# Gated linear attention with a hardswish feed-forward: alpha, k and q of three chunks loaded two tokens to a partition and turned by products

## The chip, the cores and the metric

The kernel runs on one core of one Trainium2 chip. The metric is device time in microseconds (us), the median of a few runs. The kernel before takes 530.95 us (three runs, 530.88 to 531.62).

## What is computed

```python
# attention: batch 4, 8 heads, 768 tokens, head size 48
for t in range(S):
    state = alpha[:, :, t, :, None] * state + np.einsum('bhd,bhe->bhde', k[:, :, t], v[:, :, t])
    y[:, :, t] = np.einsum('bhd,bhde->bhe', q[:, :, t], state)
# then, on 3072 tokens of 384 numbers
h = x @ w_in                       # 384 x 2048
g = h * np.clip(h + 3.0, 0.0, 6.0) / 6.0
return g @ w_out                   # 2048 x 384
```

The inputs alpha, k, q and v lie in memory as batch, head, token, head element, in float32. One token of one head is therefore a run of 48 numbers, 192 bytes, and the next token of the same head follows it directly. The two weight matrices come as float64 and are rounded to float32 on the chip from their bits.

## The kernel before

The tokens are worked off in 24 chunks of 128, six to a batch entry. For one chunk, alpha, k and q are wanted with the head elements along the partitions: a pair of heads takes 128 partitions (64 for each head, 48 of them used), four pairs stand side by side, and the 128 tokens run along the free axis. In memory the tokens come first, so each of the three has to be turned.

For chunks 0 to 5 (`FIRST = 6`) this is done on TensorE. `load_akq` (L253, its DMA at L256) fetches one tensor of one chunk with one DMA, token by token: partition s holds token s, eight heads of 64 columns each, of which 48 are filled with a run of 192 bytes. The other 16 columns hold a constant that is set once (L91: one for alpha, zero for k and q). The buffers are a ring of three for each tensor (`rings`). `transposed` (L276, the instruction at L284) then turns it with four transposes of 128 by 128, each for a pair of heads, into one bank of PSUM. From chunk 6 on, loads of runs of 640 and 768 bytes (L264) and transposes on VectorE (L288) take their place.

What follows for one chunk: ScalarE copies the turned alpha out of PSUM (`place_alpha`, L302). VectorE makes two running products of it with scans (L311 `decay`, L322 `growth`) and multiplies the turned k and q by them (`scaled`, L334). TensorE turns k back to token order (`k_by_token`, L393), ScalarE copies that (L397). Products of k with v give the update of the state (`update`, L452), which VectorE adds (L460, L462); ScalarE puts the state into its place (L438). Products of k with q give the scores (L365), VectorE masks them (L375), and `attend` (L478) makes the chunk's result, which ScalarE copies out (L487) for the feed-forward (L512, L501, L539 for the first tokens, L623 and L726 later).

Two features set the order. First, everything stands in one list written out by hand (from L774), with `manual_schedule`; each engine gets its instructions in that order and works them in that order. A word names a step and its arguments. The list begins:

```python
z.0.5 z.0.3 z.0.1 qa.0.0 w.0 d2.0 d3.0 la.0 ta.0.0 z.0.8 lk.0 tk.0.1 la.1 ta.1.2
lq.0 tq.0.3 lk.1 lv.0.0 d1.0 ca.0 r.0 p.0 k.0 kb.0.0 z.0.2 z.0.2 q.0 la.2 dx.0 ca.1
r.1 ck.0 u.0.2.1 sm.0.0 qa.0.1 sv.0.1 tk.1.0 p.1 sc.0.2.3 w.2 lq.1 sm.0.1 k.1 m.0
ta.2.0 z.0.2 d1.2 ca.2 d2.2 kb.1.0 ck.1 r.2 tq.1.2 q.1 dx.2 lv.1.1 u.1.3.1 z.0.3
```

Here `la`, `lk`, `lq` and `lv` are the loads of alpha, k, q and v, and `w` one of 768 KB of weights. `ta`, `tk` and `tq` are the turns. `ca` is the copy of alpha, `r` and `p` the scans, `k` and `q` the products of L334. `kb` and `ck` bring k back to token order, `u` is the update. `sc` and `m` are scores and mask, `d1` to `d4` the rounding of weights. `z.0.8` is eight products of the identity with itself that nobody reads (`idle`, L555). The last number of a turn is its PSUM bank.

Second, all loads and stores are issued by SyncE (SP), one after the other. Each DMA signals one of eight semaphores, taken in turn, and the issue of a DMA waits until the DMA that had this semaphore before, eight issues earlier, has landed.

Of the kernel before, what the change touches and what calls it, by code (L numbers as in the profile page):

```python
# [17 lines left out]
def kernel(  # L18
# [32 lines left out]
    nc = tc.nc  # L51
    B, H, S, D = q.shape
# [10 lines left out]
    HB = C // 2  # L63
# [9 lines left out]
    ident = consts.tile([C, C], FP, tag="ident")  # L73
# [10 lines left out]
    NR = 3  # L84
    NV = 3
    ring = {}
    rings = consts.tile([C, 3 * NR, H, 64], FP, tag="rings")
    for r in range(NR):
        for name, pad in (("a", 1.0), ("k", 0.0), ("q", 0.0)):
            t = ring[name, r] = rings[:, 3 * r + "akq".index(name)]  # L90
            (nc.vector if r == 0 else nc.gpsimd).memset(t[:, :, D:64], pad)  # L91

    vs, As = [], []
    for r in range(NV):
        t = consts.tile([C, 2, H, 64], FP, tag=f"v{r}", name=f"v{r}")
# [10 lines left out]
    for r in range(2):  # L106
        t = consts.tile([C, NP * W + 1], FP, tag=f"ax{r}")
        nc.vector.memset(t, 0.0)
        aX.append(t)
        t = consts.tile([C, NP * W], FP, tag=f"ini{r}")  # L110
# [118 lines left out]
    def bank(name, j, i):  # L229
        ps_t[name, j] = banks[i].rearrange("r (p n) -> r p n", p=NP)  # L230
        return ps_t[name, j]
# [7 lines left out]
    for r in range(NQ):  # L239
        for name in "akq":  # L240
            quads[name, r] = consts.tile([C, NP, V, D], FP, tag=f"{name}q{r}",
                                         name=f"{name}q{r}")

    def rows(t, j):
        b, c = divmod(j, NC)
        return t[b, :, c * C : (c + 1) * C, :]

    def pad(r):
        for name in "akq":
            for o in (BLK, 3 * BLK):  # L250
                nc.gpsimd.memset(quads[name, r][o : o + BLK, :, V - 1, D - BLK : BLK], 1.0)

    def load_akq(name, j):  # L253
        src = rows({"a": alpha, "k": k, "q": q}[name], j)
        if j < FIRST:
            nc.sync.dma_start(out=ring[name, j % NR][:, :, 0:D],  # L256
                              in_=src.rearrange("h s d -> s h d"))
            return
        to = quads[name, j % NQ]
        to = to.rearrange("r p v d -> r p (v d)")  # L260
        t = src.rearrange("(p a) (u v) d -> a u p (v d)", a=2, v=V)
        for o in range(4):
            skip = BLK * (o % 2)
            nc.sync.dma_start(out=to[BLK * o : BLK * (o + 1), :, 0 : V * D - skip],  # L264
                              in_=t[o // 2, :, :, skip : V * D])
# [10 lines left out]
    def transposed(name, j, i=None):  # L276
        if j >= FIRST:
            t = (K_t if name == "k" else Q_t)[j] = (Ks if name == "k" else Qs)[j % 2]
            by_blocks(t, name, j)
            return  # L280
        t = bank("t" + name, j, i)
        src = ring[name, j % NR]
        for p in range(NP):
            nc.tensor.transpose(  # L284
                t[:, p], src[:, 2 * p : 2 * p + 2].rearrange("s h d -> s (h d)"), ident)

    def by_blocks(to, name, j):
        nc.vector.transpose(out=to.rearrange("r p (u v) -> r p v u", v=V),  # L288
                            in_=quads[name, j % NQ][:, :, :, 0:BLK])
# [305 lines left out]
    for i in range(8):  # L595
        r, o = divmod(i, 3)
# [70 lines left out]
    t = {1: b[0, 1], 2: spare[:, 0], 3: spare[:, 1], 4: spare[:, 2]}  # L667
# [76 lines left out]
    def store2(g, i):  # L744
# [5 lines left out]

    steps = {
        "la": lambda j: load_akq("a", j), "lk": lambda j: load_akq("k", j),
        "lq": lambda j: load_akq("q", j), "lv": load_v, "pd": pad, "w": load_weight,
        "d1": round_low, "d2": magnitude, "dx": sign, "d3": high_bits, "d4": add_low,
        "ta": lambda j, *i: transposed("a", j, *i), "tk": lambda j, *i: transposed("k", j, *i),
        "tq": lambda j, *i: transposed("q", j, *i), "ca": place_alpha, "r": decay, "p": growth,
        "k": lambda j: scaled("k", j), "q": lambda j: scaled("q", j),
        "sc": scores, "m": masked, "sp": scores_of_two, "mp": masked_two, "up": update_two, "qa": place_q, "kb": k_by_token, "ck": keep_k,
# [197 lines left out]
```

## Time and profile before

| | |
|---|---|
| median of 3 runs | 530.95 us |
| the profiled execution | 531.43 us |
| its span (first to last instruction) | 529.6 us |
| TensorE (PE) busy | 519.6 us, 98% of the span |
| VectorE (DVE) busy | 471.4 us, 89% |
| ScalarE (ACT) busy | 256.9 us, 48% |
| GpSimd (POOL) busy | 49.2 us, 9% |
| granted clock of TensorE | 1.00 in every stage |
| DMA | 124,100 packets, 54.40 MB, mean 103 GB/s |
| loads of alpha, k, q into the ring (L256) | 18 DMAs of 192 KB |

PE is TensorE's matmul and PEld its weight loads. In a list of instructions the columns are start, duration, engine, line, operation, output and input, count, and in brackets the idle time before it with what ended it. A matmul's recorded duration reaches past the start of the next one, so the time that it takes up is read from the distance of starts. A product in float32 stands there as two matmuls, a transpose as one.

### The profile page before, as it was taken

The page shows a single profiled execution, that of the slowest core. Times are in us where ns is not written, and L with a number is a line of the kernel's source. Part 1 is how long each engine was busy: PE and PEld are TensorE (multiplying, and loading weights), DVE is VectorE, ACT ScalarE, POOL GpSimd, SP SyncE. Part 2 cuts the span into 40 slices and gives each one's busy share as a digit, 9 for nine tenths or more (in the row PEclk, how much of TensorE's full clock was granted, in tenths as well). Part 3 has the DMA queues.
Part 4 walks back from the last instruction along what each step waited for, and adds up shares of the span by engine and source line. Part 5 has one row for each costly group of instructions (what it writes and reads, how often), then busy time and mean ns, then how long its engine had stood idle before and what let it go on. Part 6 is the DMA issues. An engine that isn't in the chain of part 4 may idle for free.

```text
span 529.6 us, 15031 instructions
## 1 busy us (share of the span) xinstructions
PE 519.6 (98%) x6300; PEld 496.0 (94%) x6300; DVE 471.4 (89%) x817; ACT 256.9 (48%) x503; POOL 49.2 (9%) x71
## 2 busy tenths in 40 slices
PE   7899999999999999999999999999999999999997
PEld 6688887789999999999999999999999999999997
DVE  7999999999999999999999999999999996376381
ACT  5789867013564443553353562554344534443320
POOL 7323343100000000000000000001000000000000
PEclk9999999999999999999999999999999999999999
DMA  9999989300416535456415356463435041000011
GB/s 172 221 251 266 249 239 198 71 15 1 106 22 139 125 81 118 117 123 139 100 30 133 85 108 152 95 138 87 83 82 123 15 77 37 2 24 1 1 39 45
DMA packets 124100, 54.40 MB, mean 103 GB/s; under 512 B 83328, under 2 KB 116864, under 8 KB 124032
## 3 DMA queue, kind: packets, MB, share of 16 engines
q1 hardware_dynamic: 124032, 53.44, 44.8%
q8 instruction: 49, 0.80, 0.7%
q14 instruction: 19, 0.16, 0.1%
HBM read 44.50 MB, written 8.91 MB: 101 GB/s over the span
## 4 chain that ended last, share of the span: by engine, by line
PE 87%; DVE 7%; DMA 2%; ACT 2%; issue 1%; POOL 0%; SPq 0%; DVEq 0%; ACTq 0%
PE m_ps L726 36%; PE m_ps L623 33%; PE m_ps L501 6%; PE m_ps L539 4%; PE t_ps L478 4%; PE t_ps L365 2%; PE t_ps L452 2%; DMA v<-in_v_dram 1%; DMA rings<-in_alpha_dram 1%; DVE R L311 1%; DVE A L353 1%; ACT raw L191 1%; DVE k L288 1%; PE m_ps L512 1%; DVE k L334 0%
## 5 line engine op out<-in xcount | busy, mean ns | idle before, releaser
L726 PE MATMUL m_ps<-w,g_sb 128*128 128x192 f32 x704 | 122.2, 327 | 0.0
L629 ACT COPY g_sb<-m_ps 128x512 f32<-128x512 f32 x110 | 63.6, 583 | 110.7 <-PE m_ps L623 82.5
L726 PEld LDWEIGHTS m_ps<-w,g_sb 128*128 128x128 f32 x704 | 113.9, 190 | 0.7
L726 PE MATMUL m_ps<-rings,g_sb 128*128 128x192 f32 x528 | 91.3, 326 | 0.0
L726 PEld LDWEIGHTS m_ps<-rings,g_sb 128*128 128x128 f32 x528 | 85.4, 190 | 0.0
L623 PE MATMUL m_ps<-xc,w 128*128 128x128 f32 x640 | 83.2, 278 | 0.4 <-DVE oh L742 0.2
L517 ACT ACTIVATE r<-g_sb,half 128x512 f32<-128x512 f32 x80 | 57.2, 723 | 47.2 <-DVE g_sb L564 19.0
L623 PEld LDWEIGHTS m_ps<-xc,w 128*128 128x128 f32 x640 | 77.5, 191 | 1.8 <-DVE oh L742 0.4
L521 DVE SCALAR_TENSOR_TENSOR g_sb<-r,g_sb 128x512 f32<-128x512 f32 x80 | 54.0, 683 | 6.3 <-ACT r L517 5.3
L623 PE MATMUL m_ps<-xT,raw 128*128 128x128 f32 x400 | 52.5, 277 | 0.0
L623 PEld LDWEIGHTS m_ps<-xT,raw 128*128 128x128 f32 x400 | 48.5, 192 | 0.2
L670 DVE TENSOR_TENSOR g_sb<-g_sb 128x512 f32<-128x512 f32 (+1 forms) x55 | 41.9, 788 | 2.8 <-PE m_ps L726 2.7
L428 POOL TENSOR_TENSOR st<-sm,R 128x192 f32<-128x192 f32 x20 | 11.9, 595 | 342.4 <-DVE sm L462 338.5
L385 ACT COPY A<-q 48x256 f32<-48x256 f32 x88 | 35.5, 404 | 14.6 <-DVE q L334 13.3
L623 PE MATMUL m_ps<-xT,w 128*128 128x128 f32 x320 | 42.0, 277 | 0.0
L623 PEld LDWEIGHTS m_ps<-xT,w 128*128 128x128 f32 x320 | 38.9, 192 | 0.2 <-ACT g_sb L629 0.2
L501 PE MATMUL m_ps<-xT,w 128*128 128x256 f32 x144 | 32.6, 382 | 0.0
L623 PE MATMUL m_ps<-xc,raw 128*128 128x128 f32 x240 | 32.1, 277 | 0.0
L311 DVE TENSOR_TENSOR_SCAN R<-t,ones 128x516 f32<-128x516 f32 x24 | 29.9, 1247 | 0.4 <-ACT t L302 0.3
L501 PEld LDWEIGHTS m_ps<-xT,w 128*128 128x128 f32 x144 | 26.8, 190 | 3.6
L623 PEld LDWEIGHTS m_ps<-xc,raw 128*128 128x128 f32 x240 | 29.9, 191 | 0.3
L560 DVE TENSOR_TENSOR g_sb<-g_sb 128x512 f32<-128x512 f32 x40 | 26.9, 682 | 3.4 <-ACT g_sb L629 3.1
(105 smaller groups left out, 716.9 us busy)
## 6 DMA issues: line engine op xcount, KB each, us to landing
raw<-in_moe_w_out_dram SPq DMA_DIRECT2D x8, 768.0 KB, 5.4
raw<-in_moe_w_in_dram SPq DMA_DIRECT2D x6, 768.0 KB, 6.9
v<-in_v_dram SPq DMA_DIRECT2D x48, 96.0 KB, 3.4
out_dram<-oh SPq DMA_DIRECT2D x44, 96.0 KB, 1.8
far<-kq SPq DMA_DIRECT2D x64, 64.0 KB, 2.2
kb<-far SPq DMA_DIRECT2D x64, 64.0 KB, 2.1
qq<-in_q_dram SPq DMA_DIRECT2D x36, 96.0 KB, 2.6
aq<-in_alpha_dram SPq DMA_DIRECT2D x36, 96.0 KB, 2.7
```

Source lines behind the costliest of these rows:

```text
L311: nc.vector.tensor_tensor_scan(out=reverse(R, n - 1, n), data0=reverse(ax, n, n), data1=reverse(ones, n, n), initial=0.0, op0=ALU.mult, op ...
L385: nc.scalar.copy(out=to[:, a], in_=Q_t[j][64 * a : 64 * a + D, :, half])
L478: nc.tensor.matmul(y_of(j, (i + 1) // 2, p)[:, HB * b : HB * b + HB], vb[:, p, e : e + 32], A_t[j][:, b, 2 * p + a], start=(b == 0 and i = ...
L501: nc.tensor.matmul(h[:, f], w1[:, kk, o : o + C], xT_t[g][:, kk], start=(kk == 0), stop=(kk == KT - 1))
L517: nc.scalar.activation(out=to, in_=h, func=AF.Relu, bias=half, scale=1.0 / 6.0)
L521: nc.vector.scalar_tensor_tensor(out=to, in0=r, scalar=1.0, in1=h, op0=ALU.min, op1=ALU.mult)
L539: nc.tensor.matmul(o_t[c], gs[0][:, f, c * C : (c + 1) * C], w2[:, f], start=(f == 0), stop=(f == NF - 1))
L560: eng.tensor_tensor(out=out, in0=in0, in1=in1, op=ALU.add if s1 > 0 else ALU.subtract)
L623: nc.tensor.matmul(acc[g][i][:, f * C : (f + 1) * C], spots[w][:, f * C : (f + 1) * C], x_of(g, x), start=(first and f == 0), stop=last, s ...
L629: nc.scalar.copy(out=slots[z], in_=acc[g][i])
L670: nc.vector.tensor_tensor(out=out, in0=in0, in1=in1, op=ALU.subtract)
L726: nc.tensor.matmul(to[g], a, rhs[:, f], start=(first and f == 0), stop=(last and f == HF - 1), skip_group_check=True)
```

## The change

For chunks 0, 1 and 2 (`PAIRS`), alpha, k and q are loaded two tokens to a partition: token 2u and 2u+1 of a head go together, as one run of 384 bytes, to partition u (heads 0 to 3) or 64+u (heads 4 to 7). This is one DMA for each group of four heads, so two DMAs of 96 KB take the place of one of 192 KB, with 512 runs in the place of 1024. A partition now holds 384 numbers side by side, and the constant columns stand behind them (the memset at L91 has the same size and another place).

The turn of such a tensor is no longer four transposes but eight products with the identity. Each has 64 columns of the loaded data as its stationary operand (48 of one head and one token parity, and 16 that belong to what follows and are not used), and the identity of 128 columns as its moving one. Its result has 64 partitions and 128 columns: two groups of four heads, 64 token pairs each. It is written to every second column of the PSUM bank, so that the bank is laid out as it was. Consecutive products go to the lower and the upper 64 partitions in turn. Everything that reads the bank is as before, and so is the list. Chunks 3 to 5 keep the old load and the old turn.

```diff
             t = ring[name, r] = rings[:, 3 * r + "akq".index(name)]
-            (nc.vector if r == 0 else nc.gpsimd).memset(t[:, :, D:64], pad)
+            (nc.vector if r == 0 else nc.gpsimd).memset(t[:, 6:8], pad)
...
+    PAIRS = {("a", 0), ("k", 0), ("q", 0), ("a", 1), ("k", 1), ("q", 1), ("a", 2), ("k", 2), ("q", 2)}
+
     def load_akq(name, j):
         src = rows({"a": alpha, "k": k, "q": q}[name], j)
+        if (name, j) in PAIRS:
+            to = ring[name, j % NR].rearrange("r h e -> r (h e)")
+            t = src.rearrange("(g i) (u x) d -> g u i (x d)", g=2, x=2)
+            for g in range(2):
+                nc.sync.dma_start(
+                    out=to[HB * g : HB * g + HB, 0 : 8 * D].rearrange("u (i e) -> u i e", i=4),
+                    in_=t[g])
+            return
         if j < FIRST:
             nc.sync.dma_start(out=ring[name, j % NR][:, :, 0:D],
                               in_=src.rearrange("h s d -> s h d"))
...
         t = bank("t" + name, j, i)
         src = ring[name, j % NR]
+        if (name, j) in PAIRS:
+            flat = src.rearrange("s h e -> s (h e)")
+            for n in range(2):
+                for x in range(2):
+                    for a in range(2):
+                        to = t[64 * a : 64 * a + 64].rearrange("r (g n) (u x) -> r n x g u", g=2, x=2)
+                        o = D * (2 * (2 * n + a) + x)
+                        nc.tensor.matmul(to[:, n, x], flat[:, o : o + 64], ident,
+                                         start=True, stop=True)
+            return
         for p in range(NP):
             nc.tensor.transpose(
```

## Prediction

> **What bounds the kernel now.** First the slices of the whole span (the page's second part), then the chain of waits of the start, then the instructions in order of time.
>
> ```profile
> PE   7899999999999999999999999999999999999997
> DVE  7999999999999999999999999999999996376381
> DMA  9999989300416535456415356463435041000011
> ```
>
> A slice is 13 us. PE is full from the third slice on, so what happens in the first two decides when this full stretch begins. DMA is full there too, which makes shorter loads look welcome. The busy times in stretches of 5 us (PE, PEld, DVE, ACT, POOL, clock, DMA share, GB/s) ask whether anyone waits for them:
>
> ```profile
> 10.00:15.00 5.00, 4.19 (x87) 3.38 (x85) 4.96 (x7) 2.63 (x7) 4.36 (x12) 1.00 1.30 236
> 15.00:20.00 5.00, 2.55 (x26) 1.93 (x18) 4.79 (x10) 3.73 (x6) 0.85 (x4) 1.00 1.28 220
> 20.00:25.00 5.00, 4.96 (x149) 4.57 (x150) 4.23 (x9) 3.85 (x9) 1.34 (x1) 1.00 1.12 210
> ```
>
> From 10 to 20 us DVE is busy 9.75 of 10 us: DVE bounds the start, not DMA. The chain of waits shows the one place where a load counts after the first:
>
> ```profile
> 13.08 6.92 DMA v<-in_v_dram
> 20.00 0.04 issue
> 20.04 0.57 PE t_ps L452 x30
> ```
>
> The second half of v of chunk 1 lands at 20.00, PE waits for it, and DVE for PE:
>
> ```profile
> 6.97 0.63 PE L284 MATMUL t_ps<-ident,rings 128*128 128x128 f32 x4 [1.54 <-DMA rings<-in_alpha_dram]
> 7.44 1.95 PE L555 MATMUL m_ps<-ident 128*128 128x128 f32 x16
> 9.23 1.04 PE L284 MATMUL t_ps<-ident,rings 128*128 128x128 f32 x8
> ...
> 10.59 0.63 PE L284 MATMUL t_ps<-ident,rings 128*128 128x128 f32 x4 [0.32 <-DMA rings<-in_q_dram]
> ...
> 11.47 0.68 DVE L334 TENSOR_TENSOR q<-t_ps,P 128x512 f32<-128x512 f32 x1
> 12.07 1.64 DVE L311 TENSOR_TENSOR_SCAN R<-t,ones 128x516 f32<-128x516 f32 x1
> ...
> 17.73 1.23 DVE L311 TENSOR_TENSOR_SCAN R<-t,ones 128x516 f32<-128x516 f32 x1
> ...
> 19.21 0.69 DVE L334 TENSOR_TENSOR q<-t_ps,P 128x512 f32<-128x512 f32 x1
> ...
> 20.72 0.36 DVE L462 TENSOR_TENSOR s<-t_ps,st 128x192 f32<-128x192 f32 x1 [0.81 <-PE t_ps L452]
> ```
>
> From 6.57 to 19.9 DVE goes from one instruction to the next; its only long gap is this 0.81. The chain then runs through PE and ACT to 29.7, DVE to 42.8, and PE to the end. A delay of DVE before 19.9, or of PE behind 20, is paid in full.
>
> **The change, part by part.**
>
> *Loads.* The ring loads land at 6.84, 8.05, 9.24, 10.45 and 11.64 (the trace's landing records): one per 1.20 us, 64 packets of 192 bytes on each of 16 DMA engines, 18.8 ns each. 384 bytes stand nowhere in this trace. A packet's median is 15 ns at 192 bytes, 32 at 640 and 36 at 768; the line through these gives 22. Bounds: 15 (as for 192 bytes) and 37.6 (twice 18.8, no gain in time). I take 22, since 192 and 640 enclose it: 32 x 22 = 0.70 us per tensor, 0.50 less. The first alpha then lands at 6.4, the first q near 9, and v of chunk 1 some 4 us earlier, at 16.
>
> [...]
>
> *Issues.* SP gets nine more. A short issue takes 0.43 to 0.58 (L256 at 25.12, the four of L264 at 40.56 in 2.19), so 4.5 us of SP; but issues now stretched by a full queue (2.94 at 2.39) shorten, as half of the runs remain. With eight semaphores 768 KB of ring data may be under way where it was 1536. Queued behind are v and the weights. The first eight are out by 4.8, the ninth waits for the weights (landed 5.63). At half a microsecond an issue the first q lands near 9 and is needed at 11.3 (below): 2 us of cover. Cost nothing; without it, what is late at 11.3 adds in full.
>
> *Memsets.* Same size, 165 ns, done by 1.32: nothing.
>
> *Turns.* Four transposes start 109 ns apart: 0.44 us. Eight float32 products are 16 matmuls, as the idle products show (`z.0.8` is the x16 above, 112 ns apart). Each fills half the array's width. The trace has no 128 x 64 product. Its nearest row is the 128 x 32 one: L478 does 64 of 64 columns in 1.10 us, four beginning within 21 ns and the next four 56 ns later, so neighbours in different columns run beside each other. Bounds: beside each other, 16 x 0.112 / 2 = 0.90 us; one after the other, 1.79. Writing every second PSUM column also has no row: between free and twice as long, 1.79 again. I take 0.90, the L478 row being the same kind of packing and its writes going at full speed. Entering such a shape costs 93 ns (112 becomes 205 before L478 or L365), leaving it 93 (56 becomes 149). So a turn costs 0.46 more, and 0.09 on either side.
>
> [...]
>
> *The path.* Each step with what it was.
> 1. Turn of alpha 0: starts 6.4 + 0.13 + 0.09 = 6.62 (6.97). Before, the copy came 0.67 behind the start, of which 0.44 was the turn. Now 6.62 + 0.90 + 0.23 = 7.75, and with 0.59 of copy the scan starts at 8.34 (8.26): +0.1.
> 2. The idle products run from 7.61 to 9.40. Then k 0, alpha 1 and q 0 are turned in a row: 9.40 + 0.09 + 3 x 0.90 = 12.19, read at 12.42. DVE multiplied q at 11.47: **+0.95**, as the landing at 10.45 no longer binds and the turns do. The scan of 12.07 follows, and all of DVE up to k 1.
> 3. The turn of alpha 2 waits for k 1 (15.59 becomes 16.54, ends 17.22) because it needs its bank. 17.27 + 0.09 + 0.90 + 0.23 = 18.5, copy 0.57: scan at 19.1 (17.73, right behind the masks): +1.35.
> 4. k 1 back to tokens needs that copy: 19.1 to 19.54; the turn of q 1 gives 20.76 (19.21): +1.55.
> 5. Update of chunk 1: v is there, DVE adds at 21.4 (20.72): **+0.7**. The gap of 0.81 is gone; that is the change's whole return.
> 6. q 2 and k 2 are turned on a full PE (24.56): 0.92 + 0.09 more, less what DVE's k took behind its q anyway. DVE's k goes from 25.86 to some 27.2: +1.35.
> 7. The scan at 29.72 had waited 0.33 for ACT, which is only 0.7 late: **+1.0**. From there DVE, then PE, are full, and nothing gives it back.
>
> The sum is +1.0 us on the profiled execution's 531.43 (span 529.6 and 1.8 around it), so 532.4. That execution lay 0.5 over the median, so against 530.95 it is 531.9. Measurement can tell about 0.2% (1.06 us) from no change; the forecast lies just within.
>
> **The rivals.**
>
> *Turns that cost DVE nothing, so faster.* If the products took no longer than the transposes (a single pass for the identity), steps 1 to 4 and 6 fall away and the 0.81 is gained, with 0.1 more: 530.05. It decides at step 2: the three turns must be read by 11.5, so at most 0.6 us each. For it: loads do land earlier. Against it: every plain float32 product of the trace stands as two matmuls. More than 1.06 us needs more slack than the gap holds. Chance 0.18, half of it beyond 0.2%.
>
> *Halves one after the other, or writes at half speed.* 1.79 per turn. Step 1: +1.0; step 2: 10.39 + 5.37 + 0.23 = 16.0, +4.5; steps 3 and 4 add 1.0 and 1.4; step 5 gives 0.8 back; step 6 adds 2.7, less 0.33: +8.3, so 539. Against it: L478. Chance 0.13.
>
> *Loads that do not get shorter.* A packet of 384 bytes takes 37.6 ns, an engine bound by bytes in small runs. Alpha 0 lands at 6.84, step 1 and the idle products come 0.44 later, and the rest follows: +1.4, 532.4. v still comes early enough for step 5 only if the 1.4 us packet of instructions that held one DMA engine at 16 falls elsewhere. For it: 192-byte packets took 28 ns in the steady part. Against it: 640 in 32. [...] Chance 0.17.
>
> **How the numbers follow.** Forecast 0.52, rivals 0.18, 0.13, 0.17. The forecast's own spread is 531.3 to 532.6 (a turn between 0.8 and 1.0, landings within 0.3), 0.29 of it within 0.2% and 0.23 slower. The third rival gives 0.03 within and 0.14 slower; the second is slower; the first 0.09 faster and 0.09 within. So faster 0.09, within 0.41, slower 0.50. The range leaves out the second rival and most of the faster tail: 529.9 to 533.2.
>
> **What would show it.** Turns of sixteen matmuls, in pairs 112 ns apart (single ones would be the second rival, eight matmuls the first). The first alpha landed by 6.5 (6.84: third rival). DVE's first q near 12.4 with PE as its releaser, the scan of 17.73 near 19.1, no wait for v at the L462 of 20.72. Wrong would be a DMA as releaser between 7 and 20 us, or a full PE that starts no later than before.

## The result and the profile after

The changed kernel takes 537.30 us (three runs, 537.16 to 537.52), the kernel before 530.95: a ratio of 1.0116, 95% interval 1.0093 to 1.0139. It is slower by 6.3 us, where 1.0 was forecast, and lies outside the range. The profiled execution took 537.52 with a span of 535.7.

The slices of the whole span, as for before:

```profile
PE   7699999999999999999999999999999999999997
DVE  6789999999999999999999999999999986376381
DMA  8997999400306634555424355554334131000011
```

PE is full from the third slice on, as it was; but its second slice has 6 where it had 8, and DVE's first three have 6, 7 and 8 where they had 7, 9 and 9. Most of the loss is made in the first 31 us (4.7 of 6.0, by the table below). The stretches of 5 us (PE, PEld, DVE, ACT, POOL, clock, DMA share, GB/s):

```profile
10.00:15.00 5.00, 5.00 (x102) 4.66 (x100) 4.10 (x7) 2.17 (x6) 4.22 (x11) 1.00 0.85 226
15.00:20.00 5.00, 2.97 (x65) 2.30 (x59) 3.42 (x8) 2.13 (x5) 1.02 (x5) 1.00 0.94 148
20.00:25.00 5.00, 4.42 (x136) 3.67 (x136) 4.63 (x8) 4.43 (x7) 0.00 (x0) 1.00 1.27 259
25.00:30.00 5.00, 3.37 (x54) 3.19 (x56) 2.06 (x7) 4.92 (x8) 2.32 (x2) 1.00 1.24 256
```

DVE was busy 9.75 of the 10 us behind 10.00 and is now busy 7.52. Between 25 and 30, where PE should have been full, it is busy 3.37 of 5. The chain of waits names the places (start, length, what):

```profile
10.67 7.85 DMA raw<-in_moe_w_in_dram
...
19.33 0.58 ACT t L322
...
24.42 2.21 issue
```

"issue" is time in which an engine waits for nothing that the profile shows. Here it stands in the middle of one run of 32 small matmuls, the scores of chunk 1: 14 before it, 18 behind it (their lines are below). VectorE in order of time shows what each place costs:

```profile
12.62 0.69 DVE L354 TENSOR_TENSOR q<-t_ps,P 128x512 f32<-128x512 f32 x1 [0.87 <-PE t_ps L300]
...
19.93 1.23 DVE L331 TENSOR_TENSOR_SCAN R<-t,ones 128x516 f32<-128x516 f32 x1 [1.56 <-ACT t L322]
...
22.29 0.34 DVE L482 TENSOR_TENSOR s<-t_ps,st 128x192 f32<-128x192 f32 x1
...
27.23 1.53 DVE L395 TENSOR_TENSOR A<-t_ps,mask 64x256 f32<-64x256 f32 x4 [1.89 <-PE t_ps L385]
29.79 0.69 DVE L354 TENSOR_TENSOR q<-t_ps,P 128x512 f32<-128x512 f32 x1 [1.04 <-PE t_ps L300]
```

VectorE has the same 817 instructions in the same order in both kernels, so each can be held against itself. The table gives how late it starts, in us; the last column is an experiment from below.

| instruction (start before) | forecast | measured | run with three edits |
|---|---|---|---|
| first scan (8.26) | +0.1 | +0.20 | +0.37 |
| first q (11.47) | +0.95 | +1.15 | +0.37 |
| scan of chunk 2 (17.73) | +1.35 | +2.20 | +0.61 |
| q of chunk 1 (19.21) | +1.55 | +2.46 | +0.87 |
| add of the state (20.72) | +0.7 | +1.57 | +0.60 |
| masks of chunk 1 (23.70) | none given | +3.52 | +0.60 |
| k of chunk 2 (25.86) | +1.35 | +4.88 | +1.48 |
| scan (29.72) | +1.0 | +4.67 | +1.27 |
| at 194.5 | +1.0 | +5.76 | +1.39 |
| at 442 | +1.0 | +5.98 | +1.30 |

### The profile page after: what moved, and what is told of

Read it like the earlier page. It is cut to its first block, busy times and chain, and to the rows that moved or that the text cites. A ratio compares the mean times of both kernels' runs of the same rounds, so it can differ in the third digit from the quotient of the medians.

```text
span 535.7 us, 15259 instructions
## 1 busy us (share of the span) xinstructions
PE 523.8 (98%) x6408; PEld 499.8 (93%) x6408; DVE 470.9 (88%) x817; ACT 256.5 (48%) x503; POOL 49.0 (9%) x71
## 4 chain that ended last, share of the span: by engine, by line
PE 70%; DVE 21%; issue 3%; ACT 2%; SPq 2%; DMA 1%; DVEq 0%; ACTq 0%
PE m_ps L746 32%; PE m_ps L643 31%; PE t_ps L498 3%; DVE g_sb L541 2%; PE t_ps L385 2%; DVE R L331 2%; DMA raw<-in_moe_w_in_dram 1%; SPq L261 1%; PE t_ps L472 1%; DVE k L308 1%; DVE P L342 1%; DVE A L395 1%; DVE w L207 1%; DVE raw L210 1%; DVE w L208 1%
```

## The experiments

Three theories were put against each other. Theory 1: the turns alone, as in the prediction, only larger. Theory 2: nine more issues on SP put the third load of weights off, and ScalarE, which works in order, copies alpha 2 behind it. Theory 3: TensorE runs out of instructions. Medians in us, ratios to the kernel before on the same chip; a ratio is not that of the two medians and differs a little from it.

| run | median (lowest to highest) | ratio, 95% interval |
|---|---|---|
| turn_only | 539.29 (539.11 to 539.62) | 1.0159 (1.0145 to 1.0173) |
| loads_only | 531.58 (530.98 to 534.70) | 1.0023 (1.0007 to 1.0038) |
| after_shift | 534.67 (533.04 to 535.07) | 1.0067 (1.0053 to 1.0082) |
| after_ca_first | 539.64 (537.71 to 545.08) | 1.0189 (1.0146 to 1.0231) |
| before_shift168 | 532.24 (531.52 to 534.21) | 1.0025 (1.0013 to 1.0037) |
| after_again | 537.28 (536.56 to 538.92) | 1.0110 (1.0094 to 1.0126) |
| after_idle_ahead | 538.03 (537.32 to 539.10) | 1.0127 (1.0110 to 1.0144) |
| after_three | 533.08 (532.62 to 533.27) | 1.0031 (1.0019 to 1.0043) |
| after_shift8 | 540.69 (one) | |
| before_three | 533.44 (533.03 to 533.99) | 1.0045 (1.0033 to 1.0057) |
| before_reordered | 534.44 (532.06 to 535.59) | 1.0050 (1.0033 to 1.0067) |
| before_best | 537.48 (536.80 to 537.66) | 1.0119 (1.0106 to 1.0132) |
| after_40 | 537.93 (534.82 to 538.93) | 1.0098 (1.0071 to 1.0124) |
| after_40_two | 534.69 (533.10 to 536.45) | 1.0059 (1.0039 to 1.0079) |
| before_two | 531.35 (531.09 to 533.21) | 1.0002 (0.9988 to 1.0016) |
| before_v_early | 533.87 (532.51 to 535.64) | 1.0038 (1.0024 to 1.0052) |

### Loads or turns: each half of the change alone

turn_only, from the changed kernel (and the memset as before):

```diff
     def load_akq(name, j):
-        if (name, j) in PAIRS:
+        if False:
```

> The loads of before (one DMA of 192-byte runs for each tensor, constants in their old place) with the turns by products of the changed kernel. What this kernel changes in the computation: the turned alpha, k and q of chunks 0 to 2 hold the numbers in a wrong arrangement, only the time counts. TensorE's instructions are those of the changed kernel one by one, SP's those of before. Theory 1, the turns alone (the prediction's mechanism, its sizes too small): all of the +6.3 us comes from TensorE time of the turns, so 537 or a little more, with DVE late by about 4.7 us from 31 us on and no TensorE gap that nothing ends. Theory 2, SP's issues (nine more, 0.6 us each, put the third load of weights off, and ScalarE, which works in order, holds the copy of alpha 2 behind it): without the nine issues that wait goes, DVE's scan of chunk 2 is about 1.2 us earlier than in the changed kernel (18.8 instead of 19.93), and the time is about 536. Theory 3, TensorE runs out of instructions where a block of 256 of them (16 KB) ends in the middle of small products: the stream is that of the changed kernel, so the gap of 2.2 us in the scores of chunk 1 (24.2) and that of 1.3 at 193 are here too, at the same instruction; together with theory 2, 535 to 536. If the gaps hang on the crowded DMA of the changed kernel as well, they may be shorter, down to 532.4, the sum of the prediction's third rival.

loads_only, from the changed kernel:

```diff
     def transposed(name, j, i=None):
...
-        if (name, j) in PAIRS:
+        if False:
```

> The loads of the changed kernel (two DMAs of 384-byte runs) with the four transposes of before. What this kernel changes in the computation: the turned alpha, k and q of chunks 0 to 2 hold the numbers in a wrong arrangement, only the time counts. TensorE's instructions are those of before one by one. Theory 1 (turns alone): nothing is lost, at best the gap of 0.81 us before the update of chunk 1 is gained if v lands earlier: 530.1 to 531.0. Theory 2 (issues): the third load of weights lands at about 18.5 instead of 16.3, ScalarE rounds it before it copies alpha 2, and the scan of chunk 2 comes 0.9 to 1.3 us late: 531.9 to 532.3. Theory 3 (instruction blocks): the blocks end where they ended before, so no gap of TensorE without a releaser; 531 by this theory alone.

The loads alone cost 0.5 us by the medians and 1.2 by the ratio (interval 0.4 to 2.0 us); two of the eleven runs, 534.13 and 534.70, lie apart, with a mean granted clock of 0.996 and 0.994. In the profile VectorE is ahead of the kernel before by 0.45 us at the state's add, because v of chunk 1 now lands at 18.03 and the wait of 0.81 is gone, although the first turn ran at half speed there and the first q came 0.86 late. The third load of weights was issued at 10.92, later than in the changed kernel, and yet landed at 16.25. That takes the ground from theory 2: nine more issues do not make it late by themselves. The turns alone cost more than the whole change. They carry the gap, between the same two matmuls, and more:

```profile
24.00:26.00 2.00, 0.00 (x0) 0.00 (x0) 0.53 (x2) 1.94 (x5) 1.60 (x1) 0.87 1.11 168
26.00:28.00 2.00, 1.48 (x21) 1.36 (x21) 0.65 (x2) 2.00 (x3) 0.71 (x2) 0.50 0.60 112
```

These are stretches of turn_only. TensorE starts nothing from 23.38 to 26.52, and the granted clock (third column from the end) is 0.50 from 25.5 to 32.3. So the gap is paid twice: from the masks of chunk 1 to k of chunk 2 VectorE falls 3.7 us further behind, and 1.35 in the changed kernel, whose profiled execution kept a clock of 1.00 behind the gap. The mean clock of a run shows the same: 0.993 to 0.997 in the four of turn_only, 0.999 and 1.000 in the three of the changed kernel.

### Does the gap hang on the number of instructions?

In the trace, counting TensorE's weight loads, matmuls and waits from its first (number 0), the gap at 24.4 stands ahead of instruction 705 and one of 1.01 us at 193.5 ahead of 4801, which is 16 x 256 more. The queue that carries instructions shows packets of 16,384 bytes, about one for every 256 of TensorE's instructions (50 packets, 12,907 instructions). A block is here such a group of 256. after_shift:

```diff
-la.0 ta.0.0 z.0.8 lk.0
+la.0 ta.0.0 z.0.3 zs.0.24 lk.0
...
+    def small(m, n):
+        for i in range(n):
+            o = 32 * (i % 4)
+            nc.tensor.matmul(bank_m[m][o : o + 32, 0:HB], ident[:, o : o + 32], ident[:, 0:HB],
+                             start=True, stop=True)
```

> The changed kernel, with the eight idle products of the identity behind the first turn replaced by three of them and 24 small ones (32 by 64), which take about the same time (1.7 instead of 1.8 us) but are 76 more instructions of TensorE, weight loads counted. All that follows is the same, only its place against the blocks of 256 instructions is moved. Theory 3 (instruction blocks): the gaps of 2.2 us at 24.2 and of 1.3 us at 193 are gone, since no block of the shifted stream is worked off in less than 3.9 us: 533.9, and DVE is late by some 2.5 us instead of 4.7 behind 31 us. Theories 1 and 2: TensorE's small products change nothing, 537.3.

Both gaps are gone, and 2.6 us of the 6.3 with them, although in this profile the first q came 1.5 us later than in the changed kernel's (the clock, below). after_shift8, whose first number in the list is the place of the gap (`zs` is the word for `small`):

```diff
-la.0 ta.0.0 z.0.8 lk.0
+la.0 ta.0.0 z.0.8 zs.0.2 lk.0
```

> The changed kernel with two small products (32 by 64; four matmuls and four weight loads) added behind the eight idle ones, so eight more instructions of TensorE ahead of all the rest. Theory 3 (blocks of 256 instructions): the gap in the scores of chunk 1 stays where the block ends, so it moves eight instructions, four matmuls, ahead in the code: 10 matmuls of the scores before it and 22 behind it, where there were 14 and 18. In the same way the gap at 193 moves by four matmuls. If instead something that the scores themselves wait for opens the gap, it stays between 14 and 18. Its time: 537 to 539 in both cases; one look only.

TensorE in the changed kernel, then in after_shift8:

```profile
23.96 0.46 PE L385 MATMUL t_ps<-q,k 48*64 48x64 f32 x14
26.63 0.56 PE L385 MATMUL t_ps<-q,k 48*64 48x64 f32 x18 [2.21 <-issue]
```

```profile
24.89 0.44 PE L385 MATMUL t_ps<-q,k 48*64 48x64 f32 x10
27.26 0.57 PE L385 MATMUL t_ps<-q,k 48*64 48x64 f32 x22 [1.93 <-issue]
```

Eight more instructions, and the gap moves four matmuls (and their four weight loads) ahead: 10 and 22 where it was 14 and 18. The gap at 193 stays at its number, 4801, too, which is again four matmuls ahead in the code, and a third of 0.56 us opens at instruction 6849, again 8 x 256 further. Nothing that the scores read can do that; it is the end of a block of 256 instructions.

In the first 30 us of these profiles, by the DMA records of the trace, the packet of the next block starts between 1.3 us ahead of and 5.5 us behind the moment when TensorE enters the block before it. It takes 0.9 to 1.5 us, and at every gap that stands at such a number, in all profiles, the next block starts 1.2 to 1.6 us behind the packet's end. In the changed kernel the block was entered at 20.71, the packet ran from 23.69 to 25.16, and TensorE went on at 26.63. In these profiles a block of larger matmuls lasts 8 to 20 us, and no gap shows at its end; one full of update, attend and scores, whose matmuls mostly start 6 to 40 ns apart, can be worked off before (in 3.7 us here).

after_idle_ahead asks whether the gap swallows what is gained ahead of it:

```diff
-z.0.5 z.0.3 z.0.1 qa.0.0 w.0 d2.0 d3.0 la.0 ta.0.0 z.0.8 lk.0
+z.0.5 z.0.3 z.0.4 qa.0.0 w.0 d2.0 d3.0 la.0 ta.0.0 z.0.5 lk.0
```

> The changed kernel with three of the eight idle products moved from behind the first turn to ahead of it, where TensorE has 1.5 us with nothing to do; the number and order of all other instructions is the same. [...] Theory 1 (turns on DVE's path): DVE's first q, which waited 0.87 for them, comes 0.3 to 0.7 earlier, and the time falls by as much, to 536.7 to 537.0. Theory 3 (instruction blocks): the earlier start only makes the gap in the scores of chunk 1 longer, since its end is set by the fetch of the block; the masks behind it stay at 27.2 and the time at 537.3, within 0.3. [...]

It does, though not as expected. That the first q would come 0.3 to 0.7 us sooner was the author's estimate; measured at the state's add, VectorE is 0.19 us ahead of the kernel before, 1.76 better than in the changed kernel. The gap grows to 2.41 us, and the masks come at 25.66, still 1.6 sooner; the rest goes behind them (VectorE, then the clock of this run):

```profile
25.66 1.53 DVE L395 TENSOR_TENSOR A<-t_ps,mask 64x256 f32<-64x256 f32 x4 [2.08 <-PE t_ps L385]
29.83 0.69 DVE L354 TENSOR_TENSOR q<-t_ps,P 128x512 f32<-128x512 f32 x1 [2.64 <-PE t_ps L300]
```

```profile
26.00:27.00 1.00, 1.00 (x7) 1.00 (x6) 0.99 (x4) 1.00 (x2) 0.00 (x0) 0.50 1.02 385
...
28.00:29.00 1.00, 1.00 (x9) 0.89 (x10) 0.00 (x0) 0.75 (x2) 0.00 (x0) 0.50 1.42 215
```

TensorE runs at half speed from 26 to 29.3, and at q of chunk 2 VectorE stands at 29.83, where it stood at 29.79 in the changed kernel. The time is 538.03, no gain.

before_shift168 was to bring the gap into the kernel before:

```diff
-la.0 ta.0.0 z.0.8 lk.0
+la.0 ta.0.0 zs.0.50 lk.0
```

> The kernel before, its loads and transposes untouched; only the eight idle products of the identity behind the first turn are replaced by 50 small ones (32 by 64) that take about the same time (1.7 instead of 1.8 us). TensorE then has 168 more instructions ahead of the scores of chunk 1, weight loads counted: as many as the seven turns ahead of them add in the changed kernel. Theory 3 (instruction blocks of 256): the gap that nothing ends opens in the middle of the scores of chunk 1 (about 23 us), 1 to 2.5 us long, between the same two matmuls (14 on one side, 18 on the other); the first block is fetched at about 13 instead of 16.6, and the third load of weights ends 1 to 2.5 us later than its 16.27; the time is 532.5 to 534. Theories 1 (turns) and 2 (issues): nothing that they speak of is changed, 531.0.

This missed in its main point. It is slower (532.24), but no gap opens at instruction 705, though that is the same place in the scores: the block before it was entered at 18.66, two us sooner than in the changed kernel, and the next one's packet came at 17.34 already. So the end of a block inside small matmuls is not enough; the packet must be late as well. Part of the loss has another road. A packet of instructions starts at 11.02 and takes 1.48; the second half of v of chunk 0, on its way then, lands at 14.49 on the DMA engine that ends last and at 13.06 on the one before it (13.27 and 12.89 in the kernel before), and TensorE waits for it:

```profile
14.53 0.57 PE L452 MATMUL t_ps<-v,kb 64*48 64x48 f32 x30 [0.54 <-DMA v<-in_v_dram]
```

The third load of weights is held up in the same way, 17.84 and 16.04. The clock had its part in this profile too: the first turn ran at half speed, so that the first q was 0.82 late ahead of that wait, and the granted clock was 0.50 from 17.3 to 20.7. How the 1.1 us by which VectorE is late at the end divide between packet and clock is not shown.

### ScalarE's order, and the changed kernel again

after_ca_first:

```diff
-ta.2.0 z.0.2 d1.2 ca.2 d2.2
+ta.2.0 z.0.2 ca.2 d1.2 d2.2
```

> The changed kernel with two neighbouring words of its list exchanged: ScalarE copies alpha 2 before it rounds the third load of weights, not behind it. Theory 2 (issues and ScalarE's order): the copy starts when its turn is done, at about 18.1 instead of 19.3, the scan of chunk 2 comes at about 18.7 instead of 19.93, and the time falls by 0.9 to 1.3 us, to about 536.2; but if the gap in TensorE's stream at 24.2 hangs on when the DMA engines bring the instructions, it can take that back. Theory 1: the copy of alpha 2 is late because the turns are late, so no gain, 537.3. Theory 3 alone: 537.3 as well.

> The changed kernel once more, beside the others of this call. All theories: 537.2 to 537.6. If TensorE comes up to full clock only behind 10 us in this profile (in two of the five variants so far it did at 10.6, in the changed kernel at 4.6), DVE's first q comes 1 to 2 us later, and the question is how much of that the waits behind it swallow.

ScalarE in after_ca_first:

```profile
20.00 0.58 ACT L322 COPY t<-t_ps 128x512 f32<-128x512 f32 x1 [2.43 <-PE t_ps L300]
20.61 0.94 ACT L186 ACTIVATE raw<-raw 128x768 int32<-128x768 uint32 x1
```

The copy now waits for its turn alone, and VectorE's 1.56 us of waiting ahead of the scan of chunk 2 became 0.38. The time did not fall: the start was late for another reason (the first q by 3.03), and the gap is there, 1.09 us long. What the copy is worth can't be told from runs that spread from 537.71 to 545.08. after_again, the changed kernel once more with a median of 537.28, shows the reason for the late start. The same kernel's first turn, in the first profile and in this one:

```profile
6.70 1.09 PE L300 MATMUL t_ps<-ident,rings 128*64 128x128 f32 x16 [1.50 <-DMA rings<-in_alpha_dram]
```

```profile
6.70 1.98 PE L300 MATMUL t_ps<-ident,rings 128*64 128x128 f32 x16 [1.02 <-DMA rings<-in_alpha_dram]
```

Half speed: the matmuls of the idle products start 214 ns apart until 4.6 us in the one and until about 10 in the other, then 112. (The granted clock of the profile reads 1.00 in both; the distance of starts tells it.) What brings the clock up sooner in the one is not shown: both run the same idle products ahead of the first turn, and then 1.50 and 1.02 us of nothing (in brackets above). VectorE's first q is 2.74 late in after_again, and the wait for the weights (16.49 here, 18.53 in the first profile) is gone, so the two balance up to the masks of chunk 1 (3.36 late, 3.52 in the first). Behind its gap of 1.64 us the granted clock is then 0.50 from 27.2 to 30.6, VectorE is 6.1 late at 29.72 instead of 4.67, and this execution takes 538.92.

### What the change costs where no gap opens

after_three is the changed kernel with the shift, the copy first and idle products ahead; before_three is the kernel before with the same words:

```diff
-z.0.5 z.0.3 z.0.1 qa.0.0 w.0 d2.0 d3.0 la.0 ta.0.0 z.0.8 lk.0
+z.0.5 z.0.3 z.0.4 qa.0.0 w.0 d2.0 d3.0 la.0 ta.0.0 zs.0.24 lk.0
...
-ta.2.0 z.0.2 d1.2 ca.2 d2.2
+ta.2.0 z.0.2 ca.2 d1.2 d2.2
```

> The changed kernel with three edits together: 24 small products in the place of the idle ones (76 more instructions, as in the run with the shifted stream), the copy of alpha 2 ahead of the rounding of the third load of weights, and three idle products moved ahead of the first turn. Theory 3: with no gap of TensorE in the scores of chunk 1 and at 193 the two other edits count: 534.7 (the shift alone), less 0.5 to 0.9 for the copy and 0.3 to 0.9 for turns that come sooner or at full clock: 533.0 to 533.9, which leaves the turns themselves as the price of the change, about 2 to 3 us. Theory 1: 536 to 537.

> The kernel before, its loads and transposes untouched, with the same three edits as the changed kernel had in the run with three edits (24 small products in the place of the idle ones, alpha 2 copied ahead of the rounding, three idle products moved ahead of the first turn). Against that run (533.1) it gives the price of the change itself with no gap of TensorE's stream in either. Theory of the remainder: what is left are the turns, 0.46 us longer each and 0.09 at each change of shape, as in the forecast's sum: so 530.6 to 531.8 here, 1.3 to 2.3 us below the changed kernel with the same edits. If the edits themselves brought something that has nothing to do with the change, this kernel is below 530.5.

after_three takes 533.08, with all runs within 0.65 us. Its VectorE (last column of the table) is 0.60 late at the masks and 1.27 at 29.72, and keeps that. before_three was a surprise: 533.44. Up to 31 us its VectorE is 0.20 ahead of the kernel before, so the edits are not at fault there; then it loses 0.24 by 47, 0.6 by 89 and 0.8 at 456. Only the last is the end of a block, at instruction 11713, which is 45 x 256 + 193 as 705 is 2 x 256 + 193:

```profile
453.96 1.99 PE L478 MATMUL t_ps<-A,v 128*32 128x64 f32 x126
456.48 0.27 PE L478 MATMUL t_ps<-A,v 128*32 128x64 f32 x2 [0.53 <-issue]
```

The 0.6 has another releaser. A load of weights landed at 87.79 (84.34 in the kernel before), ScalarE rounded it late, VectorE waited for that, and TensorE for VectorE, at 121 and at 135, which makes TensorE 0.9 us late:

```profile
89.62 0.56 DVE L207 TENSOR_SCALAR w<-w 128x768 f32<-128x768 f32 x1 [0.73 <-ACT w L196]
```

```profile
135.87 1.38 PE L630 MATMUL m_ps<-xc,w 128*128 128x128 f32 x10 [0.38 <-DVE g_sb L571]
```

Why this load came late is not shown. So the two kernels with the same edits differ by 1.47 us at the scan of 29.72 (1.27 late and 0.20 ahead), where neither has a gap yet: that is the price of the change in its own place, read from one profile of each. The times do not show it, since before_three then loses 1.8 us more and ends 0.36 behind after_three. Three more runs set the blocks of both kernels alike, from chunk 2 on. after_40, then what after_40_two has in its place; before_two is the kernel before with the latter's edits, but `z.0.5` in the place of `z.0.3 zs.0.12`:

```diff
-la.0 ta.0.0 z.0.8 lk.0
+la.0 ta.0.0 z.0.6 zs.0.12 lk.0
```

```diff
-z.0.5 z.0.3 z.0.1 qa.0.0 w.0 d2.0 d3.0 la.0 ta.0.0 z.0.8 lk.0
+z.0.5 z.0.3 z.0.4 qa.0.0 w.0 d2.0 d3.0 la.0 ta.0.0 z.0.3 zs.0.12 lk.0
...
-ta.2.0 z.0.2 d1.2 ca.2 d2.2
+ta.2.0 z.0.2 ca.2 d1.2 d2.2
```

> The changed kernel with 40 more instructions of TensorE behind the first turn (twelve small products in the place of two idle ones, 1.75 instead of 1.8 us). The change adds 216 to 218, so the blocks of 256 now end, behind chunk 2, where they end in the kernel before, one block later. If the blocks are the cause of all that the forecast missed: no gap at 24 nor at 193, and lateness against before stays constant from 31 us on; the time is 531.0 plus what the turns and the copy of alpha 2 cost, 532.4 to 533.5. If the products themselves or the loads cost more than forecast: 534 or more, without a gap that nothing ends.

> The same 40 instructions, and two edits that take the other waits of the start away: three idle products ahead of the first turn, and alpha 2 copied ahead of the rounding. If only the turns are left: VectorE 1.2 to 1.6 us late at 31 us and no more at the end, 532.2 to 532.6 (the forecast's 531.9 plus what its steps left out). If it is 531.9 or less, the forecast's sum holds with nothing to spare; 533 or more would mean that something else still costs.

> The kernel before with the two edits alone (three idle products moved, alpha 2 copied ahead of the rounding), and no instruction more or less. Its blocks end where they did, so 530.8 to 531.1: VectorE was full there and the copy was not late. The difference to the changed kernel with 40 instructions and the same edits is then the price of the change with equal blocks; the theory says 1.2 to 1.6 us.

Half of this came true. Behind 47 us the lateness no longer grows (after_40_two: 4.24 at 47, 4.01 at 442; the changed kernel: 4.95 and 5.98), with the blocks where the kernel before has them. But the first gap was not avoided, only moved by 40 instructions, into the attend of chunk 0 (TensorE in after_40_two; in after_40 the gap stands between the same two matmuls, 2.00 us long):

```profile
22.13 1.09 PE L498 MATMUL t_ps<-A,v 128*32 128x64 f32 x58
25.49 0.31 PE L498 MATMUL t_ps<-A,v 128*32 128x64 f32 x6 [2.27 <-issue]
```

Its block was entered at 17.19, and the packet came only at 22.68. Why it came 5.5 us later there and 1.3 us ahead in before_shift168 is not settled. before_two equals the kernel before (1.0002), so copy and idle products are worth nothing to it. after_40_two is 3.34 us above before_two, where 1.2 to 1.6 were expected; the gap of 2.27 is in this.

after_40 itself missed by more, 537.93 for 532.4 to 533.5, and there the clock comes on top: in its profile the first turn ran at half speed, and the granted clock was 0.50 from 28.2 to 31.6. The mean clocks of the single runs show what such a stretch costs. It takes 0.003 off the mean, since half of 3.4 us is that share of 530. The one run of after_40 at 1.000 took 534.82, the five at 0.996 or 0.997 took 536.77 to 538.93; in after_40_two the three at 1.000 took 533.10 to 534.45, the two at 0.997 took 536.30 and 536.45.

### Can the forecast's 0.81 us be had?

before_reordered and before_best load q and v of chunk 1 ahead of the weights, the latter with the three edits; before_v_early also moves the copy of k 1 and has idle products ahead:

```diff
-sc.0.2.3 w.2 lq.1 sm.0.1
+sc.0.2.3 lq.1 lv.1.1 w.2 sm.0.1
...
-d1.2 ca.2 d2.2 kb.1.0 ck.1 r.2 tq.1.2 q.1 dx.2 lv.1.1 u.1.3.1
+ca.2 kb.1.0 ck.1 d1.2 d2.2 r.2 tq.1.2 q.1 dx.2 u.1.3.1
```

> The kernel before with three words of the list moved: q of chunk 1 and v of chunk 1 are loaded ahead of the third load of weights instead of behind it, and alpha 2 is copied ahead of that load's rounding. It takes the prediction's 0.81 us (the only long gap of VectorE in the start, waiting for v of chunk 1) without touching loads or turns. v should land at about 15.7 instead of 20.0, the weights at about 17.5 to 18.5 instead of 16.3. If the gap was worth what the prediction took: 530.1 to 530.6. If the later weights hold ScalarE and through it VectorE: 531 or a little more.

> The kernel before with the three edits and the new order of loads together, the candidate for a version faster than both. Expected 529.9 to 530.8 if v was the only thing that the start waited for and the clock is up sooner; 531 if the later weights take the gain.

> The kernel before with q and v of chunk 1 loaded ahead of the third load of weights, ScalarE's copies of alpha 2 and of k 1 ahead of that load's rounding (in the earlier trial of this order k 1 stood behind it, and TensorE waited 3.5 us), and three idle products ahead of the first turn. If VectorE's wait for v is worth what the forecast took and nothing stands behind the later weights: 530.2 to 530.5, the first kernel below the one before. If the rounding, now later, holds the scores or the state of chunk 1 (ScalarE places the state behind it): 531 to 533.

None is faster than the kernel before. In the first two TensorE waits 3.2 and 3.4 us ahead of the update, because ScalarE's copy of k 1 stands behind the rounding of the later weights, and the granted clock falls to 0.50 for 6.8 us. In the third the wait for v is gone, and VectorE adds the state 0.87 us sooner; then the rounding (L191) holds ScalarE's copy of the first result:

```profile
21.42 1.91 ACT L191 ACTIVATE raw<-raw 128x768 f16<-128x768 int32 x1
...
23.75 0.47 ACT L487 COPY xT<-t_ps 128x384 f32<-128x384 f32 x1
```

TensorE waits 2.11 us for it, until 24.27, and the granted clock is 0.50 from 24.1 to 27.5. No version here beats the kernel before; of the changed kernel, the one with three edits is the best.

## Why the prediction was wrong

Slower was the likelier side, and the forecast's size is wrong by 5.4 us.

- **Loads: right where they count, too short in size.** The median packet of 384 bytes took 22 ns over the trace, as forecast, but 28 ns while these loads ran (6 to 10 us), and the halves landed 0.44 us apart: 0.88 a tensor, not 0.70. Alpha 0 landed at 6.57 (6.4), q at 9.17 (near 9). v of chunk 1 landed at 19.50, not 16, but VectorE no longer waits for it, as step 5 said. No step is seen in the traces: the medians of 15, 22 and 32 ns for 192, 384 and 640 bytes lie on a line.
- **Issues: right that they cost nothing, wrong in size.** One took 0.60 to 0.66 us, not half a microsecond. The weights behind them were late in the profile (18.53 for 16.27), but loads_only has the same issues and lands them at 16.25. They are late where a packet of instructions starts at 12.94 (18.53), 12.75 (turn_only, 17.38), 14.26 (after_shift, 18.81) and 11.02 (before_shift168, 17.84); with packets at 15.2 or later and the order of loads as it was they end at 16.0 to 16.9, and so they do with one at 10.37, 10.95 or 11.54 and the new loads. That the packet holds up the one DMA engine that carries it is argued from these times; the trace does not name the engine.
- **Turns: right.** Sixteen matmuls, pairs 109 ns apart, 0.9 us each. The price of the change ahead of any gap, 1.47 us with the three edits on both sides, stands against the forecast's +1.0; from the masks of chunk 1 to k of chunk 2 it grows by 0.88, where step 6 had 0.65.
- **Steps 1 and 2: right** (+0.20, +1.15 for +0.1, +0.95) when the clock is up before the first turn; with a late clock the first q is 2.7 late. That the clock can be late was not in the prediction.
- **Step 3: too small by 0.85,** the copy of alpha 2 behind the late weights on ScalarE, which waited for them until 18.5: the DMA as releaser between 7 and 20 us that the prediction had named as a sign of being wrong. "Queued behind are v and the weights" was seen, but not who waits for the weights.
- **The step that failed is 6 and 7:** "+1.0. From there DVE, then PE, are full, and nothing gives it back." Nothing gave it back, but two gaps added to it that belong to no instruction: +1.95 us at the masks of chunk 1 (VectorE) and +1.3 at 194 (TensorE, 4.6 late before it and 5.9 behind it). The 216 more instructions of TensorE were counted as time (0.46 us a turn), not as a shift of all that follows against the blocks of 256, whose cost was put at nothing. The gaps make some 3.2 of the 6.0 us of the end, 1.3 to 1.5 are the change in its own place, and the rest, by difference, is the weights and the later turns of the start that the edits of after_three recover. What sets the moment at which a packet of instructions comes, and so whether the end of a block costs anything, stays open.
- **The rivals:** none of the three was it. The second's 539 is near in size (its terms add up to 8.5, not 8.3), but by turns of 1.79 us, and they took 0.9.

## What to carry to other kernels

Here an edit that gave TensorE 216 more instructions moved the end of every later block of 256 against the work. The gaps of 2.21 and 1.01 us with "issue" as their releaser were that, and the proof was to add eight instructions and see the gap move by eight. Try an edit at two or three shifts before judging it: the same change here read +6.3 us as it stood and +3.6 with 76 instructions more ahead of it. A kernel may owe part of its time to where its blocks happen to end (before_three lost 0.53 us at 456, where the kernel before has no gap), so a control with the same number of instructions, or the same edits on both sides, says more than the change alone. Even then hold the two against each other instruction by instruction: before_three lost 1.8 us far behind the change, half of it to a late load, and the times alone would have hidden the price.

## What the runs showed of the hardware that was not expected

- TensorE's instructions arrive in packets of 16,384 bytes, 0.9 to 1.9 us each, beside the data; where a block of small matmuls ends before the next one is there, TensorE stands for 0.1 to 2.9 us and goes on 1.2 to 1.6 us behind the packet's end. The gaps with "issue" in the middle of scores and attends stood at the same instruction number modulo 256 (193), in nine kernels.
- With a gap of 1.6 to 2.9 us the granted clock fell to 0.50 in five profiles: for 3.4 us (after_idle_ahead, after_again, after_40, after_shift8) or 6.8 (turn_only), though not in every one (2.21 us in the first profile of the changed kernel and 2.27 in after_40_two left it at 1.00).
- The clock at the start differs from one execution of the same kernel to the next (full speed from 4.6 us in one, from 10.1 in another): without more idle products the first turn ran at half speed in five of seven profiles of the changed kernel and its variants with new turns. With three idle products moved ahead of it, it ran at full speed, or nearly, in all seven profiles that had them.
